# Matmuls of the attention stage chained by order edges, in the order of the source

## Chip, core and metric

The kernel runs on one core of one Trainium2 chip. The metric is the time of one execution on the device in microseconds (us), of the slowest core, here the only one. Three executions of the kernel before took 940.74, 942.1 and 942.2 us; the median is 942.1 us.

## What is computed

Retention (attention with a decay in place of the softmax) over 4 batches, 8 heads, 576 positions and 64 columns per head, then two feed-forward layers over the 2304 tokens, in fp32:

```python
scores = scale * np.matmul(q, k.transpose(0, 1, 3, 2))
Dmat = np.where(rel >= 0, gamma[:, None, None] ** rel[None, :, :], 0.0)   # rel = i - j
x = (scores * Dmat) @ v                    # heads side by side: 2304 x 512
g = x @ w_gate                             # 512 x 1536
x = (g * sigmoid(g) * (x @ w_val)) @ w_out # back to 512
h = x @ w_in                               # 512 x 2048
out = np.maximum(h, 0.0) ** 2 @ w_out2     # back to 512
```

The weights arrive as 64-bit words and are converted on the chip; every operand of the feed-forward matmuls is split into a high and a low half, and a product is three matmuls (`three`: high by high, high by low, low by high).

## The kernel before

**The attention stage.** Sixteen pairs of heads (four batches by four pairs) are worked through by a loop over n = 0 to 17; a pair has five chunks of up to 128 positions, and the last is 64 wide. Iteration n does the following, in the order of the source. `load(n + 2)` issues the loads of queries and keys and of values and keys on SyncE's queue. `prep_state(n + 1)` scales keys (on VectorE for the first four pairs, on GpSimd for the others) and queries. `scores(n, chunks 0 to 3)` writes the scores of both heads to a PSUM tile of two banks, and VectorE masks them to SBUF. `apply(n - 2, False)` takes the pair of two iterations before (LAG = 2): matmuls from the running state (L463), then products of masked scores and values (L479), into one bank that ScalarE copies to `xy`. `scores(n, last chunk)` writes another two-bank tile. `states(n)` has sixteen matmul instructions (L440), whose results ScalarE and VectorE add up. `hidden1_early(n - 6)`, from n = 6 on, is one early projection: twelve matmuls of one 128-column block of the gate or value weights against the first 512 tokens. `apply(n - 2, True)` is the small apply of the last chunk: its output goes into free columns of the tile that held the last chunk's scores of pair n, so it comes after their masking, and ScalarE's small copy of it must be through before the next last scores. Between these steps, from n = 3 on, `pump` takes one step of five of the conversion of a weight (loads into two raw buffers, two instructions on ScalarE, five on VectorE, then the split); fourteen weights are converted in this stage.

**Buffers.** Queries and keys have three buffers, keys and values four, scaled queries, states and masked scores three. The load of keys and values for pair n + 2 takes the buffer of pair n - 2, free when the small apply of iteration n is done. PSUM's eight banks are two for scores, two for last scores, one for states, one for apply, and one each for gate and value projections.

**The late stage** begins with the second block of tokens; it has the rest of the first layer and the whole second layer, all in matmuls of 512 or 256 columns. The input halves of its first block take the slots of the first block's, as the last early projection frees them.

**What sets the order.** Each engine works through its own queue in order. The order in each queue is made ahead of the run by a planner, which simulates the engines with its own costs: of the instructions that are ready in its simulated time, the earliest in the source goes first. So a matmul whose operands come late by the plan is passed by later ones. An order edge binds one instruction behind another in the queue of their engine. Before the change there are such edges in `apply` only: the products stand behind the first state matmul of each of the two heads.

Of the kernel before, what the change touches and what calls it, by code (L numbers as in the profile page):

```python
# [21 lines left out]
P = 128  # L22
# [3 lines left out]
NC = -(-S // P)  # L26
# [29 lines left out]
def retention_moe_kernel(  # L56
# [11 lines left out]
    nc = tc.nc  # L68
# [18 lines left out]

    def f32(ap):
        return ap.bitcast(F32)


    units = {}
# [87 lines left out]
    def pump(k=1):  # L180
        for _ in range(k):
            if pumped["n"] < pumped["limit"]:
                pumped["n"] += 1
                next(convert, None)
# [31 lines left out]

    def three(dst, a, b, first, last):
        (ah, al), (bh, bl) = a, b
        nc.tensor.matmul(dst, ah, bh, start=first, stop=False)  # L219
        nc.tensor.matmul(dst, ah, bl, start=False, stop=False)  # L220
        nc.tensor.matmul(dst, al, bh, start=False, stop=last)  # L221

    def cut(pair, a, n):
        return tuple(x[:, a:a + n] for x in pair)
# [133 lines left out]
    with ExitStack() as st:  # L358
# [13 lines left out]
        def warm():  # L372

            one = const.tile([P, 256], F32, tag="one", name="one")
            nc.vector.memset(one, 1.0)
            ps = bank("g")
            for _ in range(WARM):
                nc.tensor.matmul(ps[:, :256], one[:, :P], one, start=True, stop=True)

        def load(n):  # L380
            b, hp = pairs[n]
# [33 lines left out]
        def scores(n, cs):  # L415

            w, nx, hp = width(cs[0]), len(cs), pairs[n][1]
            s_t[n] = ps = ps_s.tile([P, 2, 512], F32, tag=f"s{nx}", name="s")
            for x, c in enumerate(cs):
                at = slice(c * P, c * P + w)  # L420
                for h, r in enumerate(rs):
                    nc.tensor.matmul(  # L422
                        ps[:w, h, x * w:(x + 1) * w], qk_t[n][r, 1, at], qk_t[n][r, 0, at],
                        start=True, stop=True, skip_group_check=True,
                    )
            pt = p_p.tile([P, 2, nx, w], F32, tag="p", name="p_sb") if nx > 1 else p_last[n % 3]
            nc.vector.tensor_tensor(
                out=pt[:w], in0=ps[:w, :, :nx * w].rearrange("p h (c q) -> p h c q", c=nx),
                in1=mask_sb[:w, hp, :, None, :w].to_broadcast([w, 2, nx, w]), op=ALU.mult,
            )  # L430
            for x, c in enumerate(cs):
                p_t[n, c] = pt[:, :, x, :]

        def states(n):

            vt = kv_t[n]
            ps = ps_o.tile([P, NC - 1, P], F32, tag="kv", name="kvs")[:, :, :D]
            for c in range(NC - 1):
                for r in rs:
                    nc.tensor.matmul(  # L440
                        ps[r, c], vt[:, NC + c, r], vt[:, c, r], start=True, stop=True,
                        skip_group_check=True,
                    )
            sb_t[n] = sb = sb_p.tile([P, NC - 1, D], F32, tag="sb", name="sb")
            nc.scalar.copy(sb[:, 0], ps[:, 0])
            for c in range(1, NC - 1):
                nc.vector.tensor_tensor(out=sb[:, c], in0=ps[:, c], in1=sb[:, c - 1], op=ALU.add)

        def apply(n, last):

            b, hp = pairs[n]
            cs = (NC - 1,) if last else range(NC - 1)
            if last:
                bank = s_t[min(n + LAG, len(pairs) - 1)][:, 0, 256:256 + D]
            else:
                bank = ps_o.tile([P, 512], F32, tag="o", name="o")

            def dst(c):
                return bank if last else bank[:, c * P:(c + 1) * P]

            def from_state(c, r):
                at = slice((c - 1) * P, (c - 1) * P + width(c))
                return nc.tensor.matmul(  # L463
                    dst(c)[r], sb_t[n][r, c - 1], q_t[n][r, at],
                    start=(c in (1, NC - 1)), stop=False, skip_group_check=True,
                ).ins

            c0 = NC - 1 if last else 1
            with ExitStack() as after:
                for r in rs:  # L470
                    after.enter_context(tc.issue_after(from_state(c0, r)))
                if not last:
                    for c in (2, 3):
                        for r in rs:
                            from_state(c, r)
                for c in cs:
                    pt = p_t.pop((n, c))
                    for h, r in enumerate(rs):
                        nc.tensor.matmul(  # L479
                            dst(c)[r], kv_t[n][:, c, r], pt[:, h, :],  # L480
                            start=False, stop=True, skip_group_check=True,
                        )
            t0 = b * S + cs[0] * P
            nc.scalar.copy(xy[:, hp, t0:t0 + bank.shape[-1]], bank)

        warm()
        mask_sb = const.tile([P, NP, 2, P], F32, tag="mask", name="mask_sb")
        ks_sb = const.tile([P, NP, NC - 1, 2, 1], F32, tag="ks", name="ks_sb")
# [6 lines left out]
        for n in range(last + 1 + LAG):  # L495
# [21 lines left out]
            if old:  # L517
                apply(n - LAG, True)
            pump(fill)


    wb_p = pool(ctx, "wb_p", 3 * F1 - WA)
# [97 lines left out]
```

## Time and profile before

| | before |
|---|---|
| median of three runs | 942.1 us |
| profiled execution | 941.55 us |
| its span, first to last instruction | 939.8 us |
| PE busy | 923.9 us (98%) |
| VectorE (DVE) busy | 475.9 us (51%) |
| ScalarE (ACT) busy | 327.8 us (35%) |
| first matmul of the late stage starts at | 127.94 us |

The span is that of one profiled execution; 1.75 us of its time lie outside. Times in the rows count from the span's start. PE is TensorE, DVE VectorE, ACT ScalarE, POOL GpSimd, SP SyncE; a "q" behind a name is that engine's sequencer. Matmuls are pipelined and their ends are modelled, so that the length in a row overlaps the next; the difference of two starts is what a group took. The bracket at the end of a row is idle time of the engine before it, and what ended it.

### The profile page before, as it was taken

How to read it: one execution, taken by the hardware profiler on the slowest of the kernel's cores; microseconds unless marked ns; L12 is line 12 of the kernel's file. 1: busy time of each engine (PE TensorE's matmuls, PEld its weight loads, DVE VectorE, ACT ScalarE, POOL GpSimd, SP SyncE). 2: the span in 40 equal slices, each digit the busy share in tenths (PEclk: the TensorE clock that was granted, in tenths of full speed). 3: DMA queues.
4: the chain of work that ended last, by engine and by line, in shares of the span. 5: the costliest groups of instructions: out<-in, count | busy, mean ns of one | idle time of the engine just before them, and what ended most of it. 6: DMA issues, size and time to landing. Idle time of an engine off the chain costs nothing.

```text
span 939.8 us, 12500 instructions
## 1 busy us (share of the span) xinstructions
PE 923.9 (98%) x5144; PEld 769.4 (82%) x5144; DVE 475.9 (51%) x849; ACT 327.8 (35%) x597; POOL 36.5 (4%) x35
## 2 busy tenths in 40 slices
PE   8998999999999999999999999999999999999998
PEld 6776778788889998888888888888888888888897
DVE  4998677797424243223999887242224223322332
ACT  2544264554312121112665564232223222222232
POOL 2332300000000000000000000000000000000000
PEclk9999999999999999999999999999999999999999
DMA  8776433532100000001244320000001000100010
GB/s 334 270 256 236 134 111 114 155 115 90 45 0 2 1 1 1 1 1 45 85 138 135 114 90 23 0 29 17 1 1 45 1 1 1 46 0 1 8 39 23
DMA packets 22025, 63.60 MB, mean 68 GB/s; under 512 B 2256, under 2 KB 3792, under 8 KB 21968
## 3 DMA queue, kind: packets, MB, share of 16 engines
q1 hardware_dynamic: 21968, 62.81, 19.9%
q8 instruction: 40, 0.66, 0.3%
q14 instruction: 17, 0.14, 0.0%
HBM read 57.03 MB, written 5.77 MB: 67 GB/s over the span
## 4 chain that ended last, share of the span: by engine, by line
PE 83%; DVE 7%; DMA 6%; ACT 2%; issue 1%; SPq 0%; POOL 0%; POOLq 0%; ACTq 0%; DVEq 0%
PE a L220 11%; PE a L219 11%; PE a L221 11%; PE g L221 8%; PE g L219 8%; PE g L220 8%; PE v L219 8%; PE v L220 8%; PE v L221 8%; DMA raw<-in_w 4%; DVE w L158 1%; PE s L422 1%; DVE w L167 1%; DVE w L152 1%; DVE w_lo L134 1%
## 5 line engine op out<-in xcount | busy, mean ns | idle before, releaser
L253 DVE TENSOR_TENSOR h_lo<-t,h_hi 128x512 fp32r<-128x512 f32 (+1 forms) x134 | 85.2, 636 | 70.3 <-ACT h_hi L252 69.8
L252 ACT CAST h_hi<-t 128x512 fp32r<-128x512 f32 (+1 forms) x134 | 77.1, 575 | 120.1 <-DVE t L264 66.4
L221 PE MATMUL g<-xh,w_lo 128*128 128x512 f32 (+1 forms) x304 | 113.7, 374 | 1.3 <-DVE w_lo L134 1.3
L219 PE MATMUL g<-xh,w_hi 128*128 128x512 f32 (+1 forms) x304 | 113.8, 374 | 0.0
L219 PE MATMUL v<-xh,w_hi 128*128 128x512 f32 (+1 forms) x304 | 113.6, 374 | 0.0
L220 PE MATMUL v<-xl,w_hi 128*128 128x512 f32 (+1 forms) x304 | 113.5, 373 | 0.0
L220 PE MATMUL g<-xl,w_hi 128*128 128x512 f32 (+1 forms) x304 | 113.4, 373 | 0.0
L221 PE MATMUL v<-xh,w_lo 128*128 128x512 f32 (+1 forms) x304 | 113.4, 373 | 0.0
L220 PE MATMUL a<-w_lo,h_hi 128*128 128x512 f32 x288 | 112.3, 390 | 0.0
L219 PE MATMUL a<-w_hi,h_hi 128*128 128x512 f32 x288 | 112.2, 390 | 0.0
L221 PE MATMUL a<-w_hi,h_lo 128*128 128x512 f32 x288 | 109.8, 389 | 0.0
L220 PE MATMUL a<-h_lo,w_hi 128*128 128x512 f32 (+1 forms) x216 | 79.1, 366 | 0.1
L294 DVE SCALAR_TENSOR_TENSOR t<-g,t 128x512 f32<-128x512 f32 (+1 forms) x40 | 25.5, 638 | 105.5 <-ACT t L292 105.4
L221 PE MATMUL a<-h_hi,w_lo 128*128 128x512 f32 (+1 forms) x216 | 78.9, 366 | 0.0
L219 PE MATMUL a<-h_hi,w_hi 128*128 128x512 f32 (+1 forms) x216 | 77.2, 367 | 1.5 <-ACT h_hi L252 1.5
L262 DVE TENSOR_TENSOR t<-g,t 128x512 f32<-128x512 f32 (+1 forms) x54 | 34.0, 630 | 83.3 <-ACT t L260 83.1
L294 DVE SCALAR_TENSOR_TENSOR t<-v,t 128x512 f32<-128x512 f32 (+1 forms) x40 | 25.6, 639 | 92.8 <-ACT t L292 92.5
L221 PEld LDWEIGHTS g<-xh,w_lo 128*128 128x128 f32 x304 | 57.3, 188 | 11.9 <-DVE w_lo L134 1.8
L219 PEld LDWEIGHTS g<-xh,w_hi 128*128 128x128 f32 x304 | 57.3, 188 | 10.4 <-issue 0.2
L219 PEld LDWEIGHTS v<-xh,w_hi 128*128 128x128 f32 x304 | 57.3, 188 | 10.3 <-issue 0.2
L220 PEld LDWEIGHTS g<-xl,w_hi 128*128 128x128 f32 x304 | 57.3, 188 | 10.1 <-issue 0.2
L220 PEld LDWEIGHTS v<-xl,w_hi 128*128 128x128 f32 x304 | 57.3, 188 | 10.0
(88 smaller groups left out, 1499.6 us busy)
## 6 DMA issues: line engine op xcount, KB each, us to landing
raw<-in_w SPq DMA_DIRECT2D x51, 512.0 KB, 3.6
kv_sb<-in_kv SPq DMA_DIRECT2D x16, 576.0 KB, 5.4
xy<-in_w SPq DMA_DIRECT2D x17, 512.0 KB, 3.7
qk_sb<-in_qk SPq DMA_DIRECT2D x15, 576.0 KB, 6.1
out<-o_sb SPq DMA_DIRECT2D x18, 256.0 KB, 2.3
part<-part_sb SPq DMA_DIRECT2D x4, 256.0 KB, 3.0
xy<-part SPq DMA_DIRECT2D x1, 1024.0 KB, 5.4
qs_sb<-in_qscale SPq DMA_DIRECT2D x4, 224.0 KB, 7.3
```

Of the source, the lines that this page charges most:

```text
L134: nc.vector.tensor_tensor(out=lo, in0=wf, in1=f32(hi), op=ALU.subtract)
L152: ts(out=wf, in0=wf, scalar1=TINY, scalar2=HUGE, op0=ALU.max, op1=ALU.min)
L158: nc.vector.scalar_tensor_tensor(out=w, in0=high, scalar=0xC0000000, in1=w, op0=ALU.bitwise_and, op1=ALU.bitwise_or)
L167: nc.vector.tensor_tensor(out=to, in0=to, in1=lo, op=ALU.add)
L219: nc.tensor.matmul(dst, ah, bh, start=first, stop=False)
L220: nc.tensor.matmul(dst, ah, bl, start=False, stop=False)
L221: nc.tensor.matmul(dst, al, bh, start=False, stop=last)
L252: nc.scalar.copy(hi, t)
L253: nc.vector.tensor_tensor(out=lo, in0=t, in1=f32(hi), op=ALU.subtract)
L262: nc.vector.tensor_tensor(out=t, in0=g, in1=t, op=ALU.mult)
L294: nc.vector.scalar_tensor_tensor(out=t, in0=ps, scalar=0.0, in1=t, op0=ALU.max, op1=ALU.mult)
L422: nc.tensor.matmul(ps[:w, h, x * w:(x + 1) * w], qk_t[n][r, 1, at], qk_t[n][r, 0, at], start=True, stop=True, skip_group_check=True,)
```

## The change

A wrapper `matmul` issues every matmul. While its switch is on, it adds an order edge from each matmul to the one issued before it in the source. The switch goes on before the warm-up matmuls and off behind the loop of the attention stage, so that the warm-up, all of attention and the twelve early projections form one chain on TensorE; the matmuls of the late stage go through the wrapper without an edge. The two edges in `apply` go, and the function from_state is written out in place. Nothing else differs: no instruction is added, and the order on the other engines stays with the planner.

```diff
--- before.py
+++ after.py
@@ -87,6 +87,18 @@
 
     def f32(ap):
         return ap.bitcast(F32)
+
+    chain = {"on": False, "last": None}
+
+    def matmul(*args, **kw):
+
+        with ExitStack() as behind:
+            if chain["on"] and chain["last"] is not None:
+                behind.enter_context(tc.issue_after(chain["last"]))
+            m = nc.tensor.matmul(*args, **kw)
+        if chain["on"]:
+            chain["last"] = m.ins
+        return m
 
 
     units = {}
@@ -216,9 +228,9 @@
 
     def three(dst, a, b, first, last):
         (ah, al), (bh, bl) = a, b
-        nc.tensor.matmul(dst, ah, bh, start=first, stop=False)
-        nc.tensor.matmul(dst, ah, bl, start=False, stop=False)
-        nc.tensor.matmul(dst, al, bh, start=False, stop=last)
+        matmul(dst, ah, bh, start=first, stop=False)
+        matmul(dst, ah, bl, start=False, stop=False)
+        matmul(dst, al, bh, start=False, stop=last)
 
     def cut(pair, a, n):
         return tuple(x[:, a:a + n] for x in pair)
@@ -375,7 +387,7 @@
             nc.vector.memset(one, 1.0)
             ps = bank("g")
             for _ in range(WARM):
-                nc.tensor.matmul(ps[:, :256], one[:, :P], one, start=True, stop=True)
+                matmul(ps[:, :256], one[:, :P], one, start=True, stop=True)
 
         def load(n):
             b, hp = pairs[n]
@@ -419,7 +431,7 @@
             for x, c in enumerate(cs):
                 at = slice(c * P, c * P + w)
                 for h, r in enumerate(rs):
-                    nc.tensor.matmul(
+                    matmul(
                         ps[:w, h, x * w:(x + 1) * w], qk_t[n][r, 1, at], qk_t[n][r, 0, at],
                         start=True, stop=True, skip_group_check=True,
                     )
@@ -437,7 +449,7 @@
             ps = ps_o.tile([P, NC - 1, P], F32, tag="kv", name="kvs")[:, :, :D]
             for c in range(NC - 1):
                 for r in rs:
-                    nc.tensor.matmul(
+                    matmul(
                         ps[r, c], vt[:, NC + c, r], vt[:, c, r], start=True, stop=True,
                         skip_group_check=True,
                     )
@@ -458,31 +470,24 @@
             def dst(c):
                 return bank if last else bank[:, c * P:(c + 1) * P]
 
-            def from_state(c, r):
+            for c in (cs if last else range(1, NC - 1)):
                 at = slice((c - 1) * P, (c - 1) * P + width(c))
-                return nc.tensor.matmul(
-                    dst(c)[r], sb_t[n][r, c - 1], q_t[n][r, at],
-                    start=(c in (1, NC - 1)), stop=False, skip_group_check=True,
-                ).ins
-
-            c0 = NC - 1 if last else 1
-            with ExitStack() as after:
                 for r in rs:
-                    after.enter_context(tc.issue_after(from_state(c0, r)))
-                if not last:
-                    for c in (2, 3):
-                        for r in rs:
-                            from_state(c, r)
-                for c in cs:
-                    pt = p_t.pop((n, c))
-                    for h, r in enumerate(rs):
-                        nc.tensor.matmul(
-                            dst(c)[r], kv_t[n][:, c, r], pt[:, h, :],
-                            start=False, stop=True, skip_group_check=True,
-                        )
+                    matmul(
+                        dst(c)[r], sb_t[n][r, c - 1], q_t[n][r, at],
+                        start=(c in (1, NC - 1)), stop=False, skip_group_check=True,
+                    )
+            for c in cs:
+                pt = p_t.pop((n, c))
+                for h, r in enumerate(rs):
+                    matmul(
+                        dst(c)[r], kv_t[n][:, c, r], pt[:, h, :],
+                        start=False, stop=True, skip_group_check=True,
+                    )
             t0 = b * S + cs[0] * P
             nc.scalar.copy(xy[:, hp, t0:t0 + bank.shape[-1]], bank)
 
+        chain["on"] = True
         warm()
         mask_sb = const.tile([P, NP, 2, P], F32, tag="mask", name="mask_sb")
         ks_sb = const.tile([P, NP, NC - 1, 2, 1], F32, tag="ks", name="ks_sb")
@@ -518,6 +523,8 @@
                 apply(n - LAG, True)
             pump(fill)
 
+    chain["on"] = False
+
 
     wb_p = pool(ctx, "wb_p", 3 * F1 - WA)
     ps_g2 = pool(ctx, "ps_g2", 1, space=PSUM)
```

## Rows read from the trace of the kernel before

**Rows 1.** The profile page, its first part: busy time, share of the span and number of instructions of each engine.

```profile
PE 923.9 (98%) x5144; PEld 769.4 (82%) x5144; DVE 475.9 (51%) x849; ACT 327.8 (35%) x597; POOL 36.5 (4%) x35
```

**Rows 2.** Busy time by stage: start and end of the stretch, its length, busy time and number of instructions of each engine, granted TensorE clock, busy share of the DMA engines, GB/s. The stretches are cut at the first score matmul (4.91), at the first matmul of an early projection (28.40), in the third iteration with one (43.27) and at the first matmul of the late stage (127.94).

```profile
4.91:28.40 23.49, 21.11 (x294) 17.14 (x293) 16.16 (x34) 7.42 (x17) 6.10 (x5) 1.00 1.02 400
...
43.27:127.94 84.67, 79.50 (x869) 61.50 (x868) 68.68 (x125) 35.58 (x78) 24.27 (x19) 1.00 0.58 192
127.94:939.80 811.86, 806.06 (x3844) 677.98 (x3840) 376.68 (x668) 276.24 (x487) 0.00 (x0) 1.00 0.13 42
```

**Rows 3.** Who waited for whom, TensorE, over the whole span: total us, times, longest.

```profile
PE s L422 <- ACT xy L484: 3.0, 3, 1.3
...
PE s L463 <- DVE pl L427: 1.0, 2, 0.6
```

**Rows 4.** Timeline of TensorE from 47 to 55 us and at 89 us: start, length (the end is modelled), line, operation, shape of the array's tile, output form, number of instructions in a run. An fp32 matmul is two instructions, so a pair's scores are sixteen; some records are missing from the counts.

```profile
47.14 0.93 PE L422 MATMUL s<-qk_sb 64*128 64x128 f32 x10
48.00 0.69 PE L440 MATMUL kvs<-kv_sb 128*64 128x64 f32 x16
48.61 0.33 PE L463 MATMUL s<-qs,sb 64*64 64x64 f32 x4
...
49.14 0.71 PE L422 MATMUL s<-qk_sb 64*128 64x128 f32 x6
49.78 0.87 PE L463 MATMUL o<-qs,sb 64*64 64x128 f32 x12
50.58 1.09 PE L479 MATMUL o<-p_sb,kv_sb 128*64 128x128 f32 x16
51.60 0.33 PE L422 MATMUL s<-qk_sb 64*64 64x64 f32 x4
51.87 0.50 PE L221 MATMUL v<-xh,w_lo 128*128 128x512 f32 x1
...
54.83 0.93 PE L422 MATMUL s<-qk_sb 64*128 64x128 f32 x10
...
88.82 1.16 PE L422 MATMUL s<-qk_sb 64*128 64x128 f32 x16
89.91 0.33 PE L463 MATMUL s<-qs,sb 64*64 64x64 f32 x4
```

**Rows 5.** Timeline of TensorE: matmuls of the early projection of iteration 13 (tile v), and the first matmul of the late stage.

```profile
81.45 0.39 PE L221 MATMUL v<-xh,w_lo 128*128 128x512 f32 x1
...
95.98 0.50 PE L219 MATMUL v<-xh,w_hi 128*128 128x512 f32 x1
...
99.95 0.50 PE L220 MATMUL v<-xl,w_hi 128*128 128x512 f32 x1
...
127.94 0.50 PE L219 MATMUL g<-xh,w_hi 128*128 128x512 f32 x1
```

**Rows 6.** Timeline of GpSimd: the first scaling of keys that runs there, which is that of pair 4 (pairs 0 to 3 are scaled on VectorE).

```profile
28.75 1.11 POOL L398 TENSOR_TENSOR kv_sb<-kv_sb,ks_sb 128x512 f32<-128x512 f32 x1 [2.21 <-DMA kv_sb<-in_kv]
```

**Rows 7.** Timeline of TensorE from 57 to 84 us: products of the small apply (L479, output s) and scores of the last chunk (L422, 64*64).

```profile
57.09 0.34 PE L479 MATMUL s<-pl,kv_sb 128*64 128x64 f32 x4
...
62.12 0.33 PE L422 MATMUL s<-qk_sb 64*64 64x64 f32 x4 [1.34 <-ACT xy L484]
...
65.94 0.34 PE L479 MATMUL s<-pl,kv_sb 128*64 128x64 f32 x4
...
68.76 0.33 PE L422 MATMUL s<-qk_sb 64*64 64x64 f32 x4
...
75.54 0.34 PE L479 MATMUL s<-pl,kv_sb 128*64 128x64 f32 x4
...
79.02 0.33 PE L422 MATMUL s<-qk_sb 64*64 64x64 f32 x4 [0.46 <-ACT xy L484]
...
83.97 0.34 PE L479 MATMUL s<-pl,kv_sb 128*64 128x64 f32 x4
```

**Rows 8.** Timeline of VectorE: masking of the last chunk's scores (L427, output pl), and the last split of the input at the end of the early stage (L214).

```profile
56.03 0.27 DVE L427 TENSOR_TENSOR pl<-s,mask_sb 64x128 f32<-64x128 f32 x1
...
63.64 0.27 DVE L427 TENSOR_TENSOR pl<-s,mask_sb 64x128 f32<-64x128 f32 x1
...
73.20 0.27 DVE L427 TENSOR_TENSOR pl<-s,mask_sb 64x128 f32<-64x128 f32 x1
...
83.38 0.27 DVE L427 TENSOR_TENSOR pl<-s,mask_sb 64x128 f32<-64x128 f32 x1
...
129.89 0.69 DVE L214 TENSOR_TENSOR xl<-xy,xh 128x512 fp32r<-128x512 f32 x1 [1.68 <-ACT xh L213]
```

**Rows 9.** Timeline of ScalarE: one conversion of a weight (L149) and the copies of the small apply's output (L484, input s).

```profile
60.76 0.67 ACT L149 ACTIVATE raw<-raw 128x512 uint32<-128x512 uint16 x1 [2.35 <-DMA raw<-in_w]
...
61.88 0.19 ACT L484 COPY xy<-s 128x64 f32<-128x64 f32 x1
...
68.48 0.23 ACT L484 COPY xy<-s 128x64 f32<-128x64 f32 x1
...
78.75 0.22 ACT L484 COPY xy<-s 128x64 f32<-128x64 f32 x1
...
87.70 0.19 ACT L484 COPY xy<-s 128x64 f32<-128x64 f32 x1
```

**Rows 10.** Who waited for whom, SyncE's DMA queue, up to 130 us: L390 issues the load of keys and values.

```profile
SPq L390 <- PE s L479: 19.2, 8, 5.4
```

## Prediction

> **What bounds the kernel now.** I read the page first: TensorE (PE) is busy in 923.9 of 939.8 us [rows 1]. So the time falls only where PE loses idle time or does the same matmuls in less time. Then I cut the span by stages: up to 127.94 us, where the first matmul of the late stage starts [rows 5], and after it [rows 2]. After it PE is busy in 806.06 of 811.86 us and the change does not touch its instructions. The edges concern only the first 128 us. Of these, the stretch from 43.27 to 127.94 us holds 84.67 us with 79.50 us of PE work: 5.17 us idle. In that stretch VectorE (DVE) is busy 68.68 us, so no other engine is full on average; but the named waits of PE in the early stage are for DVE's and ScalarE's (ACT's) answers: 3.0 us for the small copy of the output, 1.0 us for the masked last chunk [rows 3].
>
> Next the timeline of PE, read by differences of starts, since ends are modelled. It gives a price for each group of an iteration [rows 4]: the 16 score matmuls whole 89.91 - 88.82 = 1.09 us; the state part of apply 0.80 (49.78 to 50.58); its other 16 1.02 (to 51.60); the last chunk's scores 0.27 (to 51.87); the states 0.61 (48.00 to 48.61); apply of the last chunk 0.53 (48.61 to 49.14); one projection of 12 matmuls 2.96 (51.87 to 54.83). The same rows show what the planner's order costs: scores cut into 10 and 6 take 0.86 + 0.64 = 1.50 us, 0.41 more than whole. Each return to a form of matmul costs a fixed part.
>
> **The change part by part.** No instruction is added or removed: the matmuls, copies and DMAs are the same, and order edges carry no wait between engines. The two old edges (apply's products behind its first state matmuls) are contained in the new chain. What moves is the place of each matmul in PE's queue, and with it what PE waits for and what waits for PE.
>
> (1) Groups stay whole. Between 43.27 and 127.94 us the trace has nine scores, ten last scores, ten states, eleven applies, twelve small applies and 120 projection matmuls. At the prices above: 9 x 1.09 + 10 x 0.27 + 10 x 0.61 + 11 x 1.82 + 12 x 0.53 + 10 x 2.96 = 74.6 us. PE was busy 79.5 us there, so about 4.9 us go to cutting groups and to changes between forms. In source order every group is whole and in a fixed turn; I count this 4.9 us as saved, the surest term of the sum. What the cut rows show agrees in kind with the Trainium skill, "TensorEngine Tiling (Array Packing)", section Tiling Modes: a change of tiling mode drains TensorE. By that rule alone one would count the groups that differ in tile shape, 97 in the trace against 85 in source order, and at 0.2 us, an estimate from the 0.41 us of a cut that makes two more changes, this saving would be 2.4 us and the forecast 2.5 us later.
>
> (2) The order itself. The planner ran projections ahead of their place in the source: six matmuls of the eighth were through by 81.45 us and the other six came at 95.98 and from 99.95 us, after attention had caught up [rows 5]. In source order each iteration from the seventh on has exactly one projection. How early can this run? The loads set the pace at first (the DMA engines have a share of 1.02 from 4.91 to 28.40 us [rows 2]). The fifth pair's keys are scaled on GpSimd (POOL) at 28.75 us, 1.11 us long, after a wait for their DMA [rows 6], so its states cannot start before 29.86 us. In source order only these remain then: the states 0.61 and the small apply 0.53 of iteration 4; iteration 5 without a projection, 1.09 + 0.80 + 1.02 + 0.27 + 0.61 + 0.53 = 4.32; ten iterations with one, 4.32 + 2.96 = 7.28 each; two that only apply and project, 5.31 each. Sum 0.61 + 0.53 + 4.32 + 72.8 + 10.62 = 88.9 us, end at 118.7 us if PE never waits, against 127.94: at most 9.2 us to gain. An earlier landing of that load could give up to 2 us more, a late start as much less; I take zero.
>
> (3) What PE waits for in the fixed turn. A stall is no longer filled by a later group, so I price two answers. First, the small output copy on ACT frees the bank that the next last scores write. The copy started 4.79, 2.54, 3.21 and 3.73 us after the small apply's products (57.09 to 61.88, 65.94 to 68.48, 75.54 to 78.75, 83.97 to 87.70) [rows 7, 9]. In source order the last scores come 0.26 + 1.09 + 0.80 + 1.02 = 3.17 us after those products; with 0.24 us from copy to matmul (61.88 to 62.12) the copy must start by 2.93. Excess 1.86, 0, 0.28, 0.80: mean 0.74 us. It is late because ACT works in order behind conversions that wait for weights: the one at 60.76 us had waited 2.35 us for its DMA [rows 9]. Second, DVE's masking of the last chunk started 4.43, 1.52, 4.44 and 4.36 us after the last scores (51.60, 62.12, 68.76, 79.02) [rows 4, 7, 8]; the small apply comes 0.27 + 0.61 + 2.96 = 3.84 us after them, so with the masking's own 0.27 us the limit is 3.57. Excess 0.86, 0, 0.87, 0.79: mean 0.63 us. Together at most 1.37 us per iteration. The two hardly add: a stall at one gives the other engine time. ACT and DVE are only that late while the fourteen early weights are converted, some six iterations. I take half the sum, 0.7 us, for six iterations: 4.1 us. Bounds: zero and 1.37 us in all twelve iterations (16.4 us).
>
> (4) Queues that the moved matmuls hold. On SyncE's queue the load of keys and values waits for the small apply of two pairs before, 19.2 us in eight times [rows 10], and weight loads stand behind it. In source order that apply is the last of its iteration, but the states that need the load come over one iteration (7.28 us) later, in place of the shorter distance that the plain iterations have. I cost it at nothing from the seventh iteration on, and up to 1 us before it. POOL's scaling has the same cover. If the cover is gone, the states wait, and everything on PE behind them.
>
> (5) The seam. After the last projection comes 0.53 us of small apply, then the late stage, whose input halves need the slots that this projection frees. In the trace the fourth half is made at 129.89 us, after PE had begun at 127.94 [rows 5, 8]: the planner hid it. Here the projection's 2.96 us and the apply cover most of it; I take 0.5 us, bounds 0 and 2.
>
> Sum: 118.7 + 4.1 + 0.5 = 123.3 us in place of 127.94: 4.6 us less in the profiled execution, whose own time is 941.55 us (span 939.8 us and 1.75 around it). The median of the three runs is 942.1, 0.55 above; the difference carries over, so 942.1 - 4.6 = 937.5 us.
>
> **The rivals.** (A) Forecast: whole groups are won, and part is paid back to waits; 935 to 940 us. (B) PE hardly waits: end at 118.7 us, 9.2 us less, 932.9 us. For it: at a steady one projection per iteration DVE has 7.28 us for what it does there, and much of its lateness comes from conversions pulled forward. Against it: its queue and ACT's are still ordered by the planner. (C) Gain eaten: the waits come to about 9 us, the end stays near 128 us, 942 us. For it: 68.68 of 84.67 us of DVE are work with hand-overs to ACT in between, which could set the pace whatever PE's order; that the edges bind less than they say belongs here. (D) Slower: the strict turn makes PE wait for the masking and the small copy in nearly every iteration at the full 1.37 us, with nothing of the later iterations to fill in. Place: ahead of the small apply and of the last scores. It decides from 9.2 / 1.37 = 6.7 iterations on; with ten it is 13.7 us of waits, end at 132.4, 4.5 us more: 946.6 us. For it: three of the four latenesses on each side exceed the limit. Against it: they come from the stretch in which DVE was fullest.
>
> **How the numbers follow.** A difference under 0.2% (1.9 us) is about what a measurement of this kernel cannot tell from none. Chances: A 0.44, B 0.14, C 0.18, D 0.24. Faster is A and B, 0.58; as C's and A's edges overlap I give 0.57 faster, 0.19 same, 0.24 slower. The forecast's own range is 935 to 940; the range for 8 in 10 takes in B with its bound and D up to ten iterations: 932.5 to 946.5.
>
> **What would show it.** Right: in the changed trace scores come as sixteen and projections as twelve, PE's busy time up to the late stage falls by some 5 us, and its idle time there is about that of before, on the masking and the small copy. The late stage's length stays at 811.9 us within 1 us. B would show nearly no waits on DVE or ACT after 40 us; D shows a wait of about 1 us on either in most iterations. The prediction is wrong in its footing if the first 30 us grow by several us (loads later because the applies that free their buffers are later), or if the late stage changes its length, since then the early stage was not what the edges changed.

## Result and profile after

The change makes the kernel slower: the median goes from 941.87 us (four executions, 940.74 to 942.2) to 953.45 us (four, 950.97 to 954.4), a ratio of 1.0122 with a 95% interval of 1.01 to 1.0145. The forecast was 937.5 us with a range of 932.5 to 946.5; the time lies above the range. The profiled execution of after took 950.97 us, the lowest of its four, with a span of 949.2 us; before it was 941.55 and 939.8. So 9.4 us are to be found between the two traces.

First, the same stages as [rows 2], in after. Columns: start and end, length, busy time and number of instructions of PE, PEld, DVE, ACT and POOL, granted TensorE clock, DMA share, GB/s.

```profile
4.91:137.63 132.72, 114.39 (x1297) 90.88 (x1296) 91.78 (x180) 50.13 (x109) 32.96 (x28) 0.91 0.62 217
...
20.82:51.00 30.18, 18.05 (x221) 14.64 (x217) 23.39 (x46) 13.01 (x27) 6.69 (x7) 0.77 0.75 259
51.00:58.93 7.93, 7.33 (x88) 5.76 (x84) 3.18 (x9) 4.49 (x9) 2.17 (x3) 1.00 0.69 223
58.93:137.63 78.70, 76.48 (x856) 60.05 (x852) 56.89 (x109) 31.01 (x70) 20.70 (x17) 1.00 0.49 165
137.63:949.20 811.57, 805.43 (x3844) 678.11 (x3840) 376.90 (x669) 276.68 (x487) 0.00 (x0) 1.00 0.13 42
```

The late stage keeps its length (811.57 against 811.86 us), but begins at 137.63 in place of 127.94: all of the loss, 9.69 us, is in the early stage. Most of it sits in one place. From the scores of iteration 3 (20.82) to those of iteration 6 (51.00) three iterations without a projection take 30.18 us, of which PE is busy 18.05, at a mean granted clock of 0.77. By the prices of the prediction they take 3 x 4.32 = 13.0 us. From 51.00 on things run nearly as priced.

Who waited for whom on PE, over the whole span of after, in the columns of [rows 3] (L98 is the wrapper, so all matmuls have this line; L439 is the masking, L459 an addition of states):

```profile
PE s L98 <- DVE pl L439: 10.6, 3, 5.2
PE s L98 <- DMA qk_sb<-in_qk: 2.0, 3, 1.6
PE kvs L98 <- DVE kv_sb L410: 1.3, 1, 1.3
PE kvs L98 <- DVE sb L459: 1.2, 1, 1.2
```

The masking of the last chunk had cost 1.0 us [rows 3]; it now costs 10.6. The timeline of PE in after shows where (columns as in [rows 4]):

```profile
20.82 1.16 PE L98 MATMUL s<-qk_sb 64*128 64x128 f32 x16
21.91 0.87 PE L98 MATMUL o<-qs,sb 64*64 64x128 f32 x12
22.71 1.09 PE L98 MATMUL o<-p_sb,kv_sb 128*64 128x128 f32 x16
23.84 0.33 PE L98 MATMUL s<-qk_sb 64*64 64x64 f32 x4
25.42 0.69 PE L98 MATMUL kvs<-kv_sb 128*64 128x64 f32 x16 [1.25 <-DVE sb L459]
31.32 0.48 PE L98 MATMUL s<-qs,sb 64*64 64x64 f32 x4 [5.21 <-DVE pl L439]
31.73 0.48 PE L98 MATMUL s<-pl,kv_sb 128*64 128x64 f32 x4
32.14 2.08 PE L98 MATMUL s<-qk_sb 64*128 64x128 f32 x16
34.15 1.54 PE L98 MATMUL o<-qs,sb 64*64 64x128 f32 x12
...
37.67 0.69 PE L98 MATMUL kvs<-kv_sb 128*64 128x64 f32 x16 [0.59 <-issue]
43.40 0.48 PE L98 MATMUL s<-qs,sb 64*64 64x64 f32 x4 [5.04 <-DVE pl L439]
```

Each group is whole and in the order of the source, as the change says. But the small apply of iteration 3 waits 5.21 us for its masking, and that of iteration 4 5.04 us. Four waits (1.25, 5.21, 0.59, 5.04) make 12.1 us. The rest of the excess of 17.2 us is the clock: after each long wait the same groups take longer, the scores 34.15 - 32.14 = 2.01 us where [rows 4] have 1.09, the state part of apply 1.47 (to 35.62) where they have 0.80. Group by group this adds 2.0 us after the first wait and 2.8 after the second, 4.8 together; 0.3 us are left over.

Why is the masking late? VectorE in after, at the scores of iteration 3 (L164 to L179 and L146 are steps of a weight's conversion):

```profile
20.80 0.69 DVE L226 TENSOR_TENSOR xl<-xy,xh 128x512 fp32r<-128x512 f32 x1 [0.72 <-ACT xh L225]
23.61 0.43 DVE L164 TENSOR_SCALAR w<-w 128x512 f32<-128x512 f32 x1 [2.12 <-ACT w L162]
...
25.62 0.68 DVE L179 CUSTOM_DVE_ANT_0 w<-raw,w 128x1024 uint16<-128x1024 uint16 x1
...
27.28 0.68 DVE L146 TENSOR_TENSOR w_lo<-w,w_hi 128x512 fp32r<-128x512 f32 x1
27.88 1.22 DVE L439 TENSOR_TENSOR p_sb<-s,mask_sb 128x1024 f32<-128x1024 f32 x1
29.02 0.68 DVE L179 CUSTOM_DVE_ANT_0 w<-raw,w 128x1024 uint16<-128x1024 uint16 x1
30.38 0.69 DVE L146 TENSOR_TENSOR w_lo<-w,w_hi 128x512 fp32r<-128x512 f32 x1 [0.69 <-ACT w_hi L145]
30.99 0.28 DVE L439 TENSOR_TENSOR pl<-s,mask_sb 64x128 f32<-64x128 f32 x1
```

and ScalarE in after, the step that VectorE waits for at 23.61:

```profile
22.34 0.68 ACT L161 ACTIVATE raw<-raw 128x512 uint32<-128x512 uint16 x1 [1.57 <-DMA raw<-in_w]
```

and VectorE in before, at the same scores (L427 is the masking, L152 the conversion step that is L164 in after):

```profile
22.47 1.23 DVE L427 TENSOR_TENSOR p_sb<-s,mask_sb 128x1024 f32<-128x1024 f32 x1 [0.30 <-PE s L422]
23.61 0.27 DVE L427 TENSOR_TENSOR pl<-s,mask_sb 64x128 f32<-64x128 f32 x1
23.89 0.43 DVE L152 TENSOR_SCALAR w<-w 128x512 f32<-128x512 f32 x1
```

The difference to see is this. In before the masking of iteration 3 comes first and the weights behind it. In after the scores are through even earlier (by 21.91), and VectorE stands idle for 2.12 us, but the instruction at the head of its queue is a conversion that waits for ScalarE, which waits for a weight's DMA; eight conversion instructions of two weights run before the masking of chunks 0 to 3 starts at 27.88, and two more before that of the last chunk at 30.99. No edge of the change binds VectorE. Its order is the planner's, and the planner made another one around the chained matmuls. That a queue holds ready work behind unready work is what the Trainium skill says of these engines ("TensorE: Matmul & The Clock Gate", section Architectural detail: the array is 16× 32×32, not 1× 128×128: VectorE's and ScalarE's queues are strict FIFO); the 2.12 us agree.

### The profile page after: what moved, and what is told of

Read it like the earlier page. It is cut to its first block, busy times and chain, and to the rows that moved or that the text cites. A ratio compares the mean times of both kernels' runs of the same rounds, so it can differ in the third digit from the quotient of the medians.

```text
span 949.2 us, 12499 instructions
## 1 busy us (share of the span) xinstructions
PE 923.5 (97%) x5144; PEld 771.5 (81%) x5144; DVE 469.0 (49%) x849; ACT 328.1 (35%) x597; POOL 33.7 (4%) x35
## 4 chain that ended last, share of the span: by engine, by line
PE 81%; DMA 8%; DVE 7%; ACT 2%; issue 1%; SPq 1%; ACTq 0%; DVEq 0%
PE a L98 34%; PE v L98 23%; PE g L98 23%; DMA raw<-in_w 6%; DVE w L170 1%; DVE w L179 1%; DVE w_lo L146 1%; DMA qk_sb<-in_qk 1%; DVE w L164 1%; DMA part<-part_sb 1%; ACT raw L161 1%; DVE p_sb L439 1%; DVE w L168 1%; DVE w_lo L265 0%; ACT w L162 0%
## 5 line engine op out<-in xcount | busy, mean ns | idle before, releaser
L98 PE MATMUL g<-xh,w_hi 128*128 128x512 f32 (+1 forms) x304 | 114.1, 375 | 0.8 <-ACT xh L225 0.8
L98 PE MATMUL v<-xh,w_hi 128*128 128x512 f32 (+1 forms) x304 | 113.7, 375 | 0.0
L98 PE MATMUL g<-xh,w_lo 128*128 128x512 f32 (+1 forms) x304 | 113.3, 373 | 0.0
L98 PE MATMUL g<-xl,w_hi 128*128 128x512 f32 (+1 forms) x304 | 113.2, 372 | 0.0
L98 PE MATMUL v<-xh,w_lo 128*128 128x512 f32 (+1 forms) x304 | 113.2, 372 | 0.0
L98 PE MATMUL v<-xl,w_hi 128*128 128x512 f32 (+1 forms) x304 | 113.2, 372 | 0.0
L98 PE MATMUL a<-w_lo,h_hi 128*128 128x512 f32 x288 | 112.3, 390 | 0.0
L98 PE MATMUL a<-w_hi,h_hi 128*128 128x512 f32 x288 | 112.2, 390 | 0.0
L98 PE MATMUL a<-w_hi,h_lo 128*128 128x512 f32 x288 | 109.8, 389 | 0.0
L98 PE MATMUL a<-h_lo,w_hi 128*128 128x512 f32 (+1 forms) x216 | 78.9, 366 | 0.0
L98 PE MATMUL a<-h_hi,w_lo 128*128 128x512 f32 (+1 forms) x216 | 78.9, 365 | 0.0
L98 PE MATMUL a<-h_hi,w_hi 128*128 128x512 f32 (+1 forms) x216 | 77.0, 366 | 1.2 <-ACT h_hi L264 1.2
L98 PEld LDWEIGHTS g<-xh,w_hi 128*128 128x128 f32 x304 | 57.2, 188 | 11.5 <-ACT xh L225 1.2
L98 PEld LDWEIGHTS v<-xh,w_hi 128*128 128x128 f32 x304 | 57.3, 188 | 10.3 <-issue 0.2
L98 PEld LDWEIGHTS g<-xh,w_lo 128*128 128x128 f32 x304 | 57.3, 188 | 10.1
L98 PEld LDWEIGHTS v<-xh,w_lo 128*128 128x128 f32 x304 | 57.3, 188 | 10.1
L98 PEld LDWEIGHTS g<-xl,w_hi 128*128 128x128 f32 x304 | 57.3, 188 | 9.8
```

What stands on the lines that cost most here:

```text
L98: m = nc.tensor.matmul(*args, **kw)
```

## Experiments

**Theories.** M: the loss is the order of VectorE's and ScalarE's queues, conversions ahead of the maskings and copies for which the strict turn waits. Rivals (letters of their own, not those of the prediction): C: the loss is the clock, which halves after a gap and makes the next gap. F: the loss is that PE may not fill gaps with projections. L: loads come late, since the small apply frees their buffers last. D: a fixed turn costs in every iteration (as the prediction's D). Later a second question: is the chain worth anything of its own, once the queues are right? Each ratio is to executions of before from the run's own round; the median of before lay between 940.75 and 942.76 us in these rounds, so that a difference of one or two microseconds between runs of different rounds says little.

**Chain only from iteration 6, and only up to it.** A switch in the loop over n; where the chain is off, the two edges of before stand in `apply` again.

```diff
         for n in range(last + 1 + LAG):
+            chain["on"] = n >= FROM      # e2_until6: n < FROM; FROM = 6
```

> The chain starts only at iteration 6, the first one with an early projection; before that the planner is free and the two old edges in apply stand. Theory M (the loss sits in iterations 3 and 4, where VectorE's queue holds weight conversions ahead of the masking that the next chained matmul needs; the fixed turn itself is good): the first 45 us look like those of the kernel before, then 7.3 us per iteration with hardly a wait, late stage from about 120 us, 934 to 938 us. Theory D (the fixed turn costs in every iteration): 945 us or more. Theory L (loads come late because the small apply frees their buffers last): 934 to 940, as the first six iterations are free here too.

> The opposite part alone: the chain covers the warm-up and iterations 0 to 5 and ends there; from iteration 6 on the planner is free, with the two old edges in apply. Theory M: the two waits of about 5 us on the masking and the stretches at half clock stay, so the loss of the first six iterations (16 us against my count) stays and the later gain goes: 950 to 958 us. Theory D: 940 to 944 us, the loss being later.

Measured: chained from 6 on 944.01 us, ratio 1.0013 (0.9998 to 1.0028); chained up to 6 951.77 us, ratio 1.0093 (1.0064 to 1.0123). The second keeps most of the loss: it is made in the first six iterations, so D, by which it would come later, falls. Its waits are not the two of 5 us that were expected, though: projections, free there, run in between from 27.06 us on (with a wait of 1.88 us for a converted weight), and the masking then costs one wait of 1.84 us. The first missed what was expected of it: its late stage starts at 128.71 us, no gain. In its trace two waits stand at the seam, one in iteration 5, still free, and one in iteration 6, the first of the chain (timeline of PE, chain from 6 on):

```profile
32.12 1.16 PE L98 MATMUL s<-qk_sb 64*128 64x128 f32 x16 [3.15 <-DVE p_sb L439]
...
43.23 0.69 PE L98 MATMUL kvs<-kv_sb 128*64 128x64 f32 x16 [3.11 <-DVE sb L459]
```

The planner's order of before has the same kind of late masking there: in before the scores of chunks 0 to 3 of iteration 4 were through by 26.5 us and masked from 30.33 on, behind five conversion and split instructions. PE had other work there: the rest of an apply, and from 28.40 to 32.27 us, where [rows 2] end their first stretch, nine projection matmuls with 1.33 us of idle time between them. So in before the lateness was hidden by filling. With the chain from 6 on, the same masking starts at 30.86 us, the projections stand in the chain and cannot come earlier, and PE is idle for 3.15 us. That speaks for M, with F as a condition of it.

**Maskings first.** The chain stays, and each conversion step is issued behind the last masking (an edge between VectorE's instructions). Nothing on TensorE differs from after.

```diff
     def pump(k=1):
...
-                next(convert, None)
+                with ExitStack() as behind:
+                    if masked["ins"] is not None:
+                        behind.enter_context(tc.issue_after(masked["ins"]))
+                    next(convert, None)
...
-            nc.vector.tensor_tensor(
+            masked["ins"] = nc.vector.tensor_tensor(
...
-            )
+            ).ins
```

> The whole chain, and besides each step of weight conversion stands, by an order edge on each engine's queue of VectorE alone, behind the last masking before it in the source. No instruction is added or left out. Theory M: no wait on the masking over 1 us in iterations 3 and 4, clock at full from 20 us on, late stage from about 120 us, 933 to 938 us. Theory L: the waits of 5 us stay and are put down to a DMA or to GpSimd's scaling in place of VectorE: 948 us or more. Theory C (the half clock that any gap in the first 50 us brings is the main loss): 942 to 948 us.

Measured: 940.85 us, ratio 0.9983 (0.9967 to 0.9999), 12.6 us under the median of after, but above the 933 to 938 us expected under M. The two maskings of iteration 3 now start at 24.30 and 25.77 us in place of 27.88 and 30.99, and the waits for the last chunk's masking fall from 10.6 to 2.9 us. New ones come up, on ScalarE's copies of the output (L493): 2.7 and 2.2 us. They are the same thing on the other queue, a conversion that waits for its weight ahead of a copy. L falls as the cause: loads were left as they were, and the late masking and most of the loss went. Timeline of ScalarE in this run:

```profile
32.75 0.67 ACT L161 ACTIVATE raw<-raw 128x512 uint32<-128x512 uint16 x1 [3.79 <-DMA raw<-in_w]
33.33 0.56 ACT L493 COPY xy<-o 128x512 f32<-128x512 f32 x1
```

**Dummy matmuls in the gap.** The chain as in after, and ten matmuls on a constant tile ahead of the small apply of iteration 3, so that PE is not idle before it. They add work and leave nothing out.

```diff
+        def filler():
+            for ps in (bank("g"), bank("g")):
+              for _ in range(FILL // 2):          # FILL = 10
+                matmul(ps[:, :256], ones["t"][:, :P], ones["t"], start=True, stop=True)
...
+            if n == 3:
+                filler()
             if old:
                 apply(n - LAG, True)
```

> The whole chain, and ten matmuls of no use (the warm-up's, 0.43 us each at full clock) ahead of the small apply of iteration 3, where TensorE waits for 5.2 us; their results are read by nobody. The planner counts them too and may put the masking of iteration 4 a little later. Theory C: the clock stays full after that gap, the 16 scores of iteration 4 take 1.09 in place of 2.01 us, and 4 us or more come back: 946 to 950 us. Theory M: these scores get faster, but the wait of iteration 4 takes most of it back, since it ends with VectorE and not with TensorE: 950 to 955 us.

Measured: 954.04 us, ratio 1.0119 (1.0092 to 1.0146), no better than after. The clock did what was meant in this gap, and the time did not follow. Timeline of PE:

```profile
26.68 4.91 PE L99 MATMUL g<-one 128*128 128x256 f32 x20
31.97 0.33 PE L99 MATMUL s<-qs,sb 64*64 64x64 f32 x4 [0.38 <-DVE pl L448]
...
32.50 1.16 PE L99 MATMUL s<-qk_sb 64*128 64x128 f32 x16
33.59 0.87 PE L99 MATMUL o<-qs,sb 64*64 64x128 f32 x12
...
41.77 0.48 PE L99 MATMUL s<-qk_sb 64*64 64x64 f32 x4 [6.28 <-ACT xy L497]
...
46.91 0.48 PE L99 MATMUL s<-qs,sb 64*64 64x64 f32 x4 [3.61 <-DVE pl L448]
```

After the filled gap the scores take 33.59 - 32.50 = 1.09 us, as at the full clock, and the waits come back one iteration later, 6.28 and 3.61 us. The first of them follows on groups at their full price and ends with a copy on ScalarE, which stood behind a conversion that had waited 2.98 us for its weight. So C falls as what makes the waits; the half clock is a cost on top. What this cost is worth, the run does not show: the clock's record has 23.9 us at 0.50 in its early stage, as in that of after, only at other places. (The planner's order on ScalarE and VectorE moved too, so this is not a run of after with the clock alone changed.)

**Projections free.** The attention stays chained, the projections go without an edge, so that they may fill.

```diff
-        matmul(dst, ah, bh, start=first, stop=False)
+        nc.tensor.matmul(dst, ah, bh, start=first, stop=False)
```

(and so for the two others in `three`.)

> Attention and warm-up are chained in the order of the source, the early projections have no edge and may fill gaps; no edges for the conversions. Theory M: the two waits come before the first projection is ready, or are planned without it, so the time stays near that of the whole chain, 948 to 954 us. Theory F (the loss is that projections can't fill the gaps any more): 940 to 944 us.

Measured: 952.8 us, ratio 1.013 (1.0115 to 1.0146). Projection matmuls do run in the first gap (from 27.55 us), and the small apply of iteration 3 then finds its masking done. But they wait for weights themselves (0.90 and 1.58 us for the high halves), so that this apply comes at 32.52 us, against 31.32 in after; that of iteration 4 still waits 2.70 us for its masking, and the largest waits for the copies come late, 2.10 us at 78.91 and 3.69 at 120.16. F alone falls: leave to fill does not give the time back to attention in a strict turn.

**Both queues, and ScalarE's alone.** As the run with the maskings first, with a second edge: each conversion step also behind the last copy of the attention on ScalarE. The other run has this second edge only.

```diff
+                    if masked["copy"] is not None:
+                        behind.enter_context(tc.issue_after(masked["copy"]))
...
-            nc.scalar.copy(sb[:, 0], ps[:, 0])
+            masked["copy"] = nc.scalar.copy(sb[:, 0], ps[:, 0]).ins
...
-            nc.scalar.copy(xy[:, hp, t0:t0 + bank.shape[-1]], bank)
+            masked["copy"] = nc.scalar.copy(xy[:, hp, t0:t0 + bank.shape[-1]], bank).ins
```

> The whole chain; each conversion step stands behind the last masking on VectorE and also behind the last copy of attention on ScalarE that comes before it in the source. Theory M widened (conversions that wait for weights stand in ScalarE's queue, too, ahead of copies that the chain needs): the large output copy still has the first step of a conversion ahead of it, since that step stands before it in the source, so only the small copies gain: 0 to 2 us under the run with edges on VectorE alone, 938 to 941 us. If ScalarE's queue were of no account: the same as that run within 0.5 us.

> The whole chain, the conversions standing behind the last copy on ScalarE's queue alone, no edge on VectorE: there four steps of a conversion still stand ahead of each masking from iteration 3 on, but of one weight, not two. Theory M: the waits on VectorE in iterations 3 and 4 shrink with the number of steps ahead, and the time lies between the changed kernel and the run with both, 940 to 948 us. If only VectorE's queue counts: 948 us or more. If only ScalarE's counts: 935 to 937 us.

Measured: both 935.32 us, ratio 0.9946 (0.9931 to 0.9961); ScalarE's alone 937.35 us, ratio 0.9964 (0.9944 to 0.9984). Both were faster than expected; with ScalarE's edge alone the time is nearest to the 935 to 937 us of "only ScalarE's counts". With both the late stage starts at 122.88 us, and the last 76 us before it hold no wait (stages of this run, columns as above):

```profile
46.84:122.88 76.04, 76.04 (x857) 60.00 (x853) 60.59 (x119) 35.49 (x78) 20.23 (x17) 1.00 0.59 190
```

ScalarE's edge alone may do so much because VectorE's conversion steps take their input from ScalarE's, so that what is held on the one is held on the other; this was not tested apart. In that run one weight, not two, stands ahead of the masking of iteration 3, which starts at 26.58 us.

**Edges for iterations 3 to 5 only.** Both edges, switched off from n = 6 on (`masked["on"] = n < FROM`).

> The whole chain with the conversions' edges on both engines, but edges only for the steps of iterations 3 to 5; later steps are free, and in VectorE's queue as built two weights then stand ahead of one masking around iterations 5 and 6. Theory M in its narrow form (only iterations 3 and 4, which have no projection, are in danger): as the run with edges throughout, 934 to 937 us. In its wider form (wherever two weights stand ahead of a masking the chain waits, until the projections give slack): the wait comes back once, in iterations 5 or 6, 938 to 945 us.

Measured: 948.07 us, ratio 1.0071 (1.0046 to 1.0097), a miss. Where the edges end, the waits begin again. Timeline of PE in this run:

```profile
50.04 0.33 PE L98 MATMUL s<-qs,sb 64*64 64x64 f32 x4 [1.78 <-DVE pl L446]
...
58.05 0.48 PE L98 MATMUL s<-qk_sb 64*64 64x64 f32 x4 [4.50 <-ACT xy L495]
```

The copy that ended the second wait stood behind two conversions that had waited 2.56 and 2.53 us for their weights, and behind a table load and an activation of the gate (1.28 and 0.60 us), so this wait is not all the conversions'. The waits are not tied to iterations 3 and 4. Nor do conversions beside a strict turn always bring them: in after nine weights are converted behind 51.00 us, and all waits on other engines there make 2.7 us.

**Conversions one place later.** Both edges with the chain, and iteration 3 starts its conversions behind its first apply, not ahead of it (`pump(fill if n > FROM - 3 else 0)` in the first of the five places), so that each later step comes one place later, too.

> As the run with edges on both engines, and besides the first of the five conversion steps comes one place later in each iteration, behind the large output copy. Theory M widened: no conversion that waits for its weight stands ahead of a copy or masking that the chain needs soon; TensorE's waits in iterations 3 to 6 fall from about 12 us in all to 5, late stage from about 121 us, 934 to 938 us. Theory L (loads set the first 45 us): 939 to 942 us, the waits then being named after DMAs of queries or keys.

Measured: 937.3 us, ratio 0.9963 (0.9942 to 0.9984): not better than both edges alone.

**The edges without the chain.** Both edges on before, TensorE's order left to the planner; and the same with the later start of the conversions.

> The kernel before with the edges of the conversions on both engines (behind the last masking, behind the last copy), without the chain and without the shift of the steps: its partner with the chain ran in 935.3 us. If whole groups in a fixed turn are worth what I counted (4.9 us) once the queues of VectorE and ScalarE suit them: 939 to 941 us. If the chain is worth nothing of its own: 934 to 937 us. If it costs even then: under 933.5 us.

> The run before with the same edges of the conversions and the same shift by one place, but without the chain: TensorE's order is the planner's, with cut groups and projections ahead of their place. If the gain of whole groups in a fixed turn is real (5 us by my count), this is 3 us or more slower than the run with the chain and the same edges: 938 to 943 us. If the edges of the conversions bring all of it: the same time as that run within 1 us.

Measured: 934.52 us, ratio 0.9927 (0.99 to 0.9953), and 934.43 us, ratio 0.9938 (0.9923 to 0.9952). These are the lowest two; by their intervals they are not to be told apart from the chained version with both edges (935.32), and all three are faster than before. The first is where it was expected if the chain is worth nothing of its own; the second was expected slower if whole groups are worth 5 us, and is 2.9 us faster than its partner with the chain (937.3). The early stage of the first of them up to its last projections, from its trace:

```profile
4.91:122.21 117.30, 111.31 (x1296) 86.20 (x1296) 96.80 (x180) 52.26 (x111) 34.15 (x28) 0.97 0.71 244
```

and of the chained one with both edges:

```profile
4.91:122.88 117.97, 110.95 (x1298) 88.46 (x1297) 92.60 (x178) 51.05 (x110) 33.36 (x28) 0.96 0.71 243
```

PE is busy 111.31 us without the chain and 110.95 with it, where before had 114.14 us from 4.91 to 127.94. Equal busy time is not equal work, for the clock differs: of the busy time 5.6 us lie in stretches at 0.50 without the chain and 10.1 us with it. Half of that taken off, an estimate, leaves 108.5 against 105.9 us. So whole groups do save some 2.6 us of PE's work at full clock beyond the edges, and this comes out nowhere in the time: the chained kernel is idle 7.0 us in place of 6.0, and longer at the lower clock.

## Why the prediction failed

**The step that failed** is the start of part (2): "In source order only these remain then", at 29.86 us, the states and the small apply of iteration 4 and "iteration 5 without a projection, 1.09 + 0.80 + 1.02 + 0.27 + 0.61 + 0.53 = 4.32". It has PE wait for a load and for nothing else before the projections begin. Part (3) priced waits "for six iterations" with projections only, and from latenesses of before's trace. By these steps the scores of iteration 6 start at 29.86 + 0.61 + 0.53 + 4.32 = 35.3 us; they start at 51.00, 15.7 us late. The load was not what held them: the keys of pair 4 were scaled by 28.88 us in after, but PE still stood ahead of the small apply of iteration 3, waiting for a masking, and came to the states of iteration 4 at 37.67. The late stage starts 14.3 us later than the predicted 123.3. The rest of the sum was 1.4 us too dear.

Behind it lies a reading: the latenesses of masking and copy in [rows 7 to 9] were taken as VectorE's and ScalarE's own, to be carried over to any order of TensorE. They are a product of the planner, which orders all queues together. With the chain it put two weights ahead of the masking of iteration 3, which in before had been masked at once. Shown by the runs: holding the conversions behind the maskings, with TensorE untouched, gives back 12.6 us, behind the copies as well 18.1 us; and waits return where the edges end.

**Part (1), whole groups: size about right, worth wrong.** Predicted 4.9 us less busy time. As it stands PE's busy time does not fall: 114.39 us before the late stage in after, 114.14 in before. Work at the half clock hides it. In after this adds the 4.8 us above and some 4.3 in the first 20 us, which have a mean clock of 0.68:

```profile
4.91:20.82 15.91, 12.53 (x146) 10.43 (x145) 8.32 (x17) 1.63 (x4) 3.40 (x3) 0.68 1.00 389
```

In before the clock's column says 1.00 there, but the groups say otherwise (timeline of PE in before, states):

```profile
8.61 1.12 PE L440 MATMUL kvs<-kv_sb 128*64 128x64 f32 x16 [0.62 <-DVE kv_sb L398]
...
15.14 0.63 PE L440 MATMUL kvs<-kv_sb 128*64 128x64 f32 x16
```

Up to about 14 us its groups took as long as those of after at 0.50 (states 1.12 us at 13.25), some 3.7 us too much. Without these, all estimates, 105.3 us stand against 110.4, so 5.1 us less, over the whole early stage. The other count weighed there, by changes of tile shape after the Trainium skill ("TensorEngine Tiling (Array Packing)", section Tiling Modes), had given 2.4 us; the measured difference is nearer to the sum from rows. But some 2 us of the saving come with the edges on the other two queues and no chain (108.5 us), and the chain's own part has not shortened the time in any run.

**Part (3) from iteration 6 on: right in its sum.** From 51.00 to 137.63 us after takes 86.63 us against 72.8 + 10.62 = 83.4 without waits, 3.2 us over; waits and seam had been put at 4.1 + 0.5. And with both edges 76.04 us from the scores of iteration 7 on, without idle time, stand against 9 x 7.28 + 10.62 = 76.1: the prices of [rows 4] hold. With its late stage at 122.88 us that kernel is the one that the sum of 123.3 describes; the forecast would have fitted a change that also put maskings and copies first, in part by luck, for the sum has no term for the 10.2 us that its clock was at 0.50.

**Parts (4) and (5): nothing seen against them.** The first 20 us hardly grew: the scores of iteration 3 start at 20.82 us, in before at 21.27, but before had by then also done the large apply of iteration 3, so that after is some 1.4 us behind (1.82 less 0.45). In iterations 3 and 4 no wait of PE is put down to a load of keys and values.

**The clock had no term.** From 20.82 to 51.00 us it cost 4.8 us, half as much as the net loss.

**Rival D** named the right wait, a strict turn that waits for the masking, and the right sign. Its price and place were wrong: not ten waits of up to 1.37 us in iterations with projections but two of 5.21 and 5.04 us ahead of them, where nothing could fill. The prediction's rivals **B** and **C** do not fit: the waits are neither none nor just the gain.

**Open.** Why the planner ranks two weights ahead of the masking once TensorE is chained isn't in a trace; its simulated times were not looked at. The late stage's length goes from 809.5 us (edges without the chain) to 813.4 (maskings first only) with the same instructions; before and after (811.9 and 811.6) lie between. Up to 3.9 us of the differences between variants are there, and their cause was not sought.

## What to carry to other kernels

An order edge on one engine can make the planner order the others anew: before fixing a turn, list for each instruction in it whose answer it needs, and bind that producer too, ahead of work on its queue that waits for DMAs. A lateness read from a trace belongs to that trace's order; where idle time is missing, ask what filled it, for a strict turn takes the filling away first. Try the producers' edges alone: here they gave 0.7%, and a fixed order of the matmuls gave no time beyond them.

## Unexpected in the hardware

The granted clock fell within the two gaps, and stayed low while PE worked again. Stages of after, cut where the clock's record changes:

```profile
26.10:29.05 2.95, 0.01 (x1) 0.00 (x0) 2.92 (x6) 0.62 (x1) 1.04 (x1) 1.00 0.56 171
29.05:35.88 6.83, 4.56 (x38) 3.77 (x40) 5.84 (x12) 4.82 (x10) 1.14 (x1) 0.50 0.74 262
35.88:42.70 6.82, 1.89 (x36) 1.47 (x34) 5.72 (x12) 2.50 (x6) 1.07 (x1) 1.00 0.74 243
42.70:49.53 6.83, 6.13 (x52) 5.08 (x52) 5.46 (x11) 2.50 (x6) 1.13 (x1) 0.50 0.69 206
```

PE did next to nothing for the 2.95 us ahead of the first fall to 0.50 (1.2 GHz), and was busy 1.89 of 6.82 us ahead of the second. Work at 0.50 took up to twice as long: scores 2.01 us for 1.09. In the last of these rows PE was busy 6.13 of 6.83 us at the lower level: an average of busy time shows such a stretch as full, and only the clock's column, or the price of a known group, tells that it was slow. And the column can miss it: in before it reads 1.00 in the first ten microseconds of attention, where sixteen states took 1.12 us in place of 0.63.
